# An SSD scan fused with a GELU feed-forward layer on one core: the scan regrouped into twelve units of 256 tokens, two tokens per partition, with 64-row tiles and Y written into the Gram banks

## The chip, the core and the metric

One core of one Trainium2 chip runs the whole program. The metric is the device time of one execution in microseconds (us); lower is better. Three plain runs of the kernel before took 124.39, 124.88 and 125.17 us, so the median is 124.88 us.

## The reference, cut to what matters

```python
batch, H, S, D = 4, 8, 768, 32      # N = d_state = 16, chunk = 32
log_a = np.log(np.clip(a, 1e-06, 1.0))
for c in range(S // chunk):         # xc, Bc, Cc, la: the chunk's slices
    cum = np.cumsum(la, axis=-1)
    L = np.exp(cum[..., :, None] - cum[..., None, :]) * causal
    M = np.einsum('bhin,bhjn->bhij', Cc, Bc) * L
    y_intra = np.einsum('bhij,bhjd->bhid', M, xc)
    y_inter = np.einsum('bhin,bhnd->bhid', Cc, state) * np.exp(cum)[..., None]
    y[:, :, sl] = y_intra + y_inter
    Bx = np.einsum('bhjn,bhjd->bhjnd', Bc, xc) * np.exp(cum[..., -1:] - cum)[..., None, None]
    state = np.exp(la.sum(-1))[..., None, None] * state + Bx.sum(axis=2)
h = y.transpose(0, 2, 1, 3).reshape(3072, 256) @ w_in        # w_in 256 x 2048
g = 0.5 * h * (1 + np.tanh(c * (h + 0.044715 * h * h * h)))
out = g @ w_out                                              # w_out 2048 x 256
```

Inputs and output are fp32. The result does not depend on the chunk length; both kernels use chunks of 128 tokens, 24 in all, six per batch.

## The kernel before

**Tiling.** The 24 chunks form 13 units (`UNITS`): chunks 0 and 1 alone, then eleven pairs, (2,3), (4,5) and so on. For each unit the kernel computes the scan's output Y, stores it transposed in bf16 as `xm` (256 features on partitions, tokens along the row), and runs the two layers on it: stage 1 (`f_s1`, matmul at L506) makes groups of 512 columns of `h` in one of two PSUM banks `hp`, `f_gelu` (ACT, L514) empties each into `gT`, and stage 2 (`f_s2`, L523) accumulates 128 tokens x 256 outputs over 16 slices of `gT`. `f_oev` empties the result and `f_store` (L536) stores 128 KB per chunk.

**The scan.** `f_R` scans the decay products, `f_RT0` and `f_RT` transpose them with fp32 matmuls (L282, L293), and `f_recip` inverts them. B and C are multiplied by these factors once per batch (`f_mul`, L349), transposed on TensorE (`f_T`, L358), copied from PSUM (`f_E`), C is masked by head parity (`f_F`, L373), and B is transposed back (`f_N`, L379). Per unit: `f_G` (L408) makes the products of B and C, 32-row tiles, into the four banks `gb`; `f_M` (L418, DVE) multiplies them with the triangle `tri`; `f_D` (L429) makes the state's increments in an `hp` bank; `f_S` and `f_SP` (L479, L486, DVE) carry the state and spread it over the heads; `f_Y` (L451 from the state, L460 from the products) accumulates Y in the bank `yb`, both in four 32-column tiles; `f_yev` (L469, ACT) empties it.

**Loads.** All but two loads are issued by SyncE's queue (SP) in one order: a, chunk 0's B and C, batch 0's B and C (768 KB), then x by chunk and the weights. B and C of a batch are loaded as 1,024 rows of 384 bytes, x as 1,024 rows of 128 bytes per chunk. The weights go through six buffers `wf`; the cast `f_wi` (L258 on POOL, L260 on DVE) also permutes the columns of `w_in`, `f_wo` casts `w_out`.

**Order.** Each operation is a `Node` with an estimated duration, its inputs, the PSUM buffers it takes and a priority. `run_order` lays the nodes out by these estimates; the program is emitted in that order, and each engine works through its own list in order. From unit `MERGE` = 4 on, Y of one unit and D and G of the next are one node, `f_YDG`. Stage 1 and 2 have the lowest priority, so they fill what the scan leaves free. Until the first stage-2 matmul, `idle` puts matmuls on zeros (`wz`, L776) where the order foresees an idle TensorE.

Of the kernel before, what the change touches and what calls it, by code (L numbers as in the profile page):

```python
# [8 lines left out]
FP32 = mybir.dt.float32  # L9
# [84 lines left out]
def kernel(  # L94
# [9 lines left out]
):  # L104
    nc = tc.nc
# [5 lines left out]
    R6 = CPB  # L111
    NCH = batch * CPB
    HC = CPB // 2
    HS = S // 2
# [4 lines left out]
    UNITS = [[0], [1]] + [[c, c + 1] for c in range(2, NCH, 2)]  # L119
    NU = len(UNITS)  # L120

    const = ctx.enter_context(tc.tile_pool(name="const", bufs=1))
    ld = ctx.enter_context(tc.tile_pool(name="ld", bufs=batch))
    wfp = ctx.enter_context(tc.tile_pool(name="wfp", bufs=6))
    ldx = ctx.enter_context(tc.tile_pool(name="ldx", bufs=NU))
    xpool = ctx.enter_context(tc.tile_pool(name="xpool", bufs=6))
    work = ctx.enter_context(tc.tile_pool(name="work", bufs=2))
    msb = ctx.enter_context(tc.tile_pool(name="msb", bufs=4))
# [3 lines left out]
    opool = ctx.enter_context(tc.tile_pool(name="opool", bufs=6))  # L132
# [6 lines left out]

    a_t = const.tile([64, HS], FP32, name="a_t")  # L140
    a_half = [bass.AP(tensor=a.tensor, offset=a.offset + i * HS, ap=[[S, batch * H], [1, HS]])
              for i in range(2)]
    XF, X16 = {}, {}
    U = [dict() for _ in range(batch)]
    bc0 = const.tile([128, 2, H, N], FP32, name="bc0")

    def load_bc0(i, q):
        q.dma_start(out=bc0[:, i], in_=(B, C)[i][0, :, 0:Q, :].rearrange("h p n -> p h n"))

    def load_bc(b, i):  # L150
        d = U[b]
        if "bc" not in d:
            d["bc"] = ld.tile([128, 2, H, R6 * N], FP32, name="bc_t")
        nc.sync.dma_start(out=d["bc"][:, i],  # L154
                          in_=(B, C)[i][b].rearrange("h (p r) n -> p h (r n)", r=R6))

    nc.sync.dma_start(out=a_t[0:32], in_=a_half[0])
    nc.scalar.dma_start(out=a_t[32:64], in_=a_half[1])
    load_bc0(1, nc.sync)
    load_bc0(0, nc.scalar)  # L160

    wz = const.tile([128, 512], BF16, name="wz")
    nc.vector.memset(wz, 0.0)
    warm = const.tile([128, 1], FP32, name="warm")
    nc.vector.memset(warm, 0.0)  # L165
    nc.scalar.activation(warm, warm, AF.Gelu_apprx_tanh)
    ends = const.tile([64, Q], FP32, name="ends")
    nc.vector.memset(ends, 0.0)
    nc.vector.memset(ends[:, Q - 1:Q], 1.0)
    ac = const.tile([64, HS + 1], FP32, name="ac")  # L170
    nc.vector.memset(ac[:, HS:HS + 1], 0.0)
    pe1 = const.tile([64, HC], FP32, name="pe1")
    pe2 = const.tile([64, 2 * batch, HC], FP32, name="pe2")

    idf = const.tile([64, 64], FP32, name="idf")
    nc.gpsimd.memset(idf, 0.0)
    nc.gpsimd.affine_select(out=idf, in_=idf, pattern=[[-1, 64]], compare_op=ALU.not_equal,
                            fill=1.0, base=0, channel_multiplier=1)
    ident = const.tile([128, 128], BF16, name="ident")
    make_identity(nc, ident)  # L180
    bmask = const.tile([128, H * D], BF16, name="bmask")
    nc.gpsimd.memset(bmask, 1.0)
    bm3 = bmask.rearrange("p (h d) -> p h d", h=H)
    nc.gpsimd.affine_select(out=bm3, in_=bm3, pattern=[[-N, H], [0, D]],
                            compare_op=ALU.is_ge, fill=0.0, base=0, channel_multiplier=1)
    nc.gpsimd.affine_select(out=bm3, in_=bm3, pattern=[[N, H], [0, D]],
                            compare_op=ALU.is_ge, fill=0.0, base=N - 1, channel_multiplier=-1)
    tri = const.tile([128, Q], BF16, name="tri")
    make_upper_triangular(nc, tri, val=1.0, diag=True)
    tri_b = tri.rearrange("p (o q t) -> p o q t", o=1, q=1).to_broadcast([128, 4, 2, Q])  # L190

    sel8 = const.tile([64, H], FP32, name="sel8")
    nc.vector.tensor_reduce(out=sel8, in_=idf.rearrange("p (b h) -> p h b", h=H),
                            op=ALU.add, axis=mybir.AxisListType.X)
    selp = const.tile([64, H, N], FP32, name="selp")
    nc.vector.tensor_copy(out=selp, in_=sel8.rearrange("p (h o) -> p h o", o=1)
                          .to_broadcast([64, H, N]))
    m8 = const.tile([64, 2 * batch], FP32, name="m8")
    nc.gpsimd.memset(m8, 1.0)
    nc.gpsimd.affine_select(out=m8, in_=m8, pattern=[[-H, 2 * batch]], compare_op=ALU.is_ge,  # L200
                            fill=0.0, base=0, channel_multiplier=1)
    nc.gpsimd.affine_select(out=m8, in_=m8, pattern=[[H, 2 * batch]], compare_op=ALU.is_ge,
                            fill=0.0, base=H - 1, channel_multiplier=-1)
    par = const.tile([128, 2], FP32, name="par")
    bmp = bmask.rearrange("p (g e d) -> p e g d", g=4, e=2)
    for e in range(2):
        nc.vector.tensor_reduce(out=par[:, e:e + 1],
                                in_=bmp[:, e, :, 0:1].rearrange("p g o -> p (g o)"),
                                op=ALU.add, axis=mybir.AxisListType.X)
    r_t = const.tile([64, HS], FP32, name="r_t")  # L210

    rt = const.tile([128, R6, batch * H], FP32, name="rt")
    pt = const.tile([128, R6, batch * H], FP32, name="pt")
    q0 = const.tile([128, H], FP32, name="q0")
    bc0s = const.tile([128, 2, H, N], BF16, name="bc0s")
    ce0 = const.tile([128, 2, Q], BF16, name="ce0")
    bh0 = const.tile([128, Q], BF16, name="bh0")
    pend = const.tile([128, NCH], FP32, name="pend")
    WF = {}
    w_in_sb = const.tile([128, 2, d_ff], BF16, name="w_in_sb")  # L220
    w_out_sb = const.tile([128, NF, d_model], BF16, name="w_out_sb")
    xm = const.tile([128, 2, n_tokens], BF16, name="xm")


    gb = ps1.tile([128, 4, 512], FP32, name="gb")
    yb = ps1.tile([128, 512], FP32, name="yb")
    y4 = yb.rearrange("p (c w t) -> p c w t", c=2, w=2)
    rp0 = yb[:, 0:H]
    T6 = [gb[:, 2 * i, 0:S // 2].bitcast(BF16) for i in range(2)]
    T6_0 = [yb[:, 0:S // 2].bitcast(BF16), T6[1]]  # L230

    T0, DT, MT, RP = {}, {}, {}, {}
    state = {}
    gts, ops, hps, outs = {}, {}, {}, {}

    def load_x(u):
        b, c = divmod(UNITS[u][0], CPB)
        XF[u] = ldx.tile([128, 2, H, D], FP32, name="x_t")
        for k in range(len(UNITS[u])):
            nc.sync.dma_start(out=XF[u][:, k], in_=x[b, :, (c + k) * Q:(c + k + 1) * Q, :]  # L240
                              .rearrange("h p d -> p h d"))
# [11 lines left out]

    def copy(eng, o, i):
        if eng == "ACT":
            nc.scalar.activation(o, i, AF.Copy)  # L256
        elif eng == "POOL":
            nc.gpsimd.tensor_copy(out=o, in_=i)  # L258
        else:
            nc.vector.tensor_copy(out=o, in_=i)  # L260

    def f_wi(q, k0, k1, eng):
        for k in range(k0, k1):
            copy(eng, w_in_sb[:, k, q * 512:(q + 1) * 512].rearrange("d (k p) -> d k p", k=4),
                 WF[("i", q)][:, k].rearrange("d (p k) -> d k p", k=4))

    def f_wo(q, eng):
        copy(eng, w_out_sb[:, 4 * q:4 * q + 4], WF[("o", q)])


    def f_clip(i0, i1):
        nc.vector.tensor_scalar(out=ac[:, i0:i1], in0=a_t[:, i0:i1], scalar1=1e-6, scalar2=1.0,
                                op0=ALU.max, op1=ALU.min)

    def f_R(k):
        nc.vector.tensor_tensor_scan(out=r_t[:, k * Q:(k + 1) * Q][:, ::-1],
                                     data0=ac[:, k * Q + 1:(k + 1) * Q + 1][:, ::-1],
                                     data1=ends[:, ::-1], initial=1.0,
                                     op0=ALU.mult, op1=ALU.max)

    def f_RT0():
        nc.tensor.matmul(out=rp0, lhsT=r_t[0:32, 0:Q], rhs=idf[0:32, 0:H], start=True, stop=True,  # L282
                         skip_group_check=True)

    def f_RT(r0, r1):
        if r0 == 0:
            RP[1] = psh.tile([128, 512], FP32, name="hp")[:, 0:R6 * batch * H] \
                .rearrange("p (r j) -> p r j", r=R6)
        r6 = r_t.rearrange("q (p r) -> q r p", r=R6)
        for r in range(r0, r1):  # L290
            for i in range(2):
                rs = slice(32 * i, 32 * i + 32)
# [4 lines left out]
    def f_recip0():  # L297
        nc.vector.reciprocal(q0, rp0)

    def f_rtc():  # L300
        nc.scalar.activation(rt, RP[1], AF.Copy)
# [511 lines left out]
```

## Time and profile before

| What | Value |
|---|---|
| Median of three runs | 124.88 us |
| Span of the profiled execution, first to last instruction | 122.8 us |
| Around the span (the median less the span; the profile prints no other time of its own) | 2.1 us |
| TensorE matmuls busy | 114.6 us, 1506 matmuls |
| ScalarE (ACT) busy | 74.9 us |
| VectorE (DVE) busy | 68.3 us |
| GpSimd (POOL) busy | 23.0 us |
| Mean granted TensorE clock | 0.972 of full |
| DMA packets | 40,591, of which 35,904 under 512 bytes |
| Last stage-2 matmul ends, last DVE copy begins | 119.10 us |

How to read the profile: PE is TensorE, PEld its weight loads, SPq the queue of SyncE. "L506" is line 506 of the kernel before. The "chain" follows the work that ended last back to its causes and lists start, length and what. The "timeline" merges neighbouring instructions of a kind and gives start, length, engine, line and shapes. The "windows" give busy time and counts (x) by stretch. Matmuls overlap, and the time one is said to last includes its way through the array, so rates are taken from the distance between starts, which is what the chain prints.

### The profile page before, as it was taken

How to read it: one execution, taken by the hardware profiler on the slowest of the kernel's cores; microseconds unless marked ns; L12 is line 12 of the kernel's file. 1: busy time of each engine (PE TensorE's matmuls, PEld its weight loads, DVE VectorE, ACT ScalarE, POOL GpSimd, SP SyncE). 2: the span in 40 equal slices, each digit the busy share in tenths (PEclk: the TensorE clock that was granted, in tenths of full speed). 3: DMA queues.
4: the chain of work that ended last, by engine and by line, in shares of the span. 5: the costliest groups of instructions: out<-in, count | busy, mean ns of one | idle time of the engine just before them, and what ended most of it. 6: DMA issues, size and time to landing. Idle time of an engine off the chain costs nothing.

```text
span 122.8 us, 3507 instructions
## 1 busy us (share of the span) xinstructions
PE 114.6 (93%) x1506; PEld 96.2 (78%) x1506; DVE 68.3 (56%) x116; ACT 74.9 (61%) x145; POOL 23.0 (19%) x38
## 2 busy tenths in 40 slices
PE   5899978989799999999999999999999999999970
PEld 5687747778678798787879889787878888888860
DVE  3897999968849888184979672475663000000110
ACT  4025536674676677656686777865768766786310
POOL 7206967750320160122000000000000000000000
PEclk9975699999999999999999999999999999999999
DMA  3999959989799899851101101101110111100121
GB/s 52 242 266 265 328 112 370 320 191 200 128 229 221 127 235 216 145 134 48 43 0 48 43 0 48 43 0 48 43 43 5 45 43 45 45 21 22 43 90 43
DMA packets 40591, 14.09 MB, mean 115 GB/s; under 512 B 35904, under 2 KB 39040, under 8 KB 40576
## 3 DMA queue, kind: packets, MB, share of 16 engines
q1 hardware_dynamic: 39488, 13.75, 46.4%
q8 instruction: 12, 0.20, 0.7%
q10 hardware_dynamic: 1088, 0.11, 0.7%
q14 instruction: 3, 0.02, 0.1%
HBM read 10.72 MB, written 3.15 MB: 113 GB/s over the span
## 4 chain that ended last, share of the span: by engine, by line
PE 70%; SPq 18%; DMA 5%; DVE 3%; issue 1%; DVEq 0%
PE o_ps L523 29%; PE hp L506 29%; SPq L240 7%; DMA bc_t<-in_B_dram 5%; SPq L252 5%; SPq L154 4%; PE yb L523 3%; SPq L248 3%; PE gb L408 2%; PE yb L451 2%; PE yb L460 2%; PE gb L358 2%; DVE ch L260 2%; PE gb L379 1%; DVE bc L349 1%
## 5 line engine op out<-in xcount | busy, mean ns | idle before, releaser
L514 ACT ACTIVATE gT<-hp 128x512 bf16<-128x512 f32 x96 | 53.6, 596 | 24.4 <-PE hp L506 24.2
L506 PE MATMUL hp<-xm,w_in_sb 128*128 128x256 bf16 (+1 forms) x416 | 53.7, 267 | 0.9 <-POOL w_in_sb L258 0.4
L523 PE MATMUL o_ps<-w_out_sb,gT 128*128 128x256 bf16 x352 | 47.3, 273 | 0.0
L506 PEld LDWEIGHTS <-w_in_sb 128*128 128x128 bf16 x416 | 37.6, 99 | 7.7 <-issue 2.0
L523 PEld LDWEIGHTS <-gT 128*128 128x128 bf16 x384 | 37.1, 98 | 4.8 <-issue 0.4
L418 DVE TENSOR_TENSOR m<-gb,tri 128x1024 bf16<-128x1024 f32 (+1 forms) x25 | 29.1, 1173 | 1.9 <-PE gb L408 1.8
L532 DVE COPY o_sb<-o_ps 128x256 f32<-128x256 f32 x2 | 0.8, 424 | 25.6 <-PE o_ps L523 25.6
L258 POOL CAST x<-x_t 128x512 bf16<-128x512 f32 (+1 forms) x12 | 8.5, 710 | 25.0 <-DMA x_t<-in_x_dram 20.1
L479 DVE SCALAR_TENSOR_TENSOR s_new<-s_new,pend,hp 128x64 f32<-128x64 f32 x16 | 4.5, 279 | 11.5 <-PE hp L429 11.2
L776 PE MATMUL o_ps<-wz 128*128 128x128 bf16 x77 | 8.9, 267 | 1.3 <-DVE warm L165 1.3
L530 ACT ACTIVATE o_sb<-o_ps 128x256 f32<-128x256 f32 x20 | 7.7, 385 | 3.8 <-PE o_ps L523 2.1
L486 DVE SCALAR_TENSOR_TENSOR sp_new<-s_new,pend,bmask 128x256 bf16<-128x256 f32 x20 | 10.0, 506 | 0.0
L469 ACT ACTIVATE xm<-yb 128x512 bf16<-128x512 f32 (+1 forms) x13 | 7.3, 564 | 4.3 <-PE yb L460 2.1
L258 POOL CAST w_in_sb<-wf 128x512 bf16<-128x512 f32 x6 | 7.0, 1193 | 7.0 <-DMA wf<-in_moe_w_in_dram 7.0
L776 PEld LDWEIGHTS <-wz 128*128 128x128 bf16 x77 | 6.5, 122 | 1.8 <-DVE warm L165 1.2
L460 PE MATMUL yb<-m,x 128*32 128x128 bf16 x192 | 6.3, 223 | 0.6 <-DVE m L418 0.6
L373 DVE TENSOR_SCALAR ce<-ch,par 128x768 bf16<-128x768 bf16 (+2 forms) x10 | 5.9, 634 | 0.8 <-ACT ch L256 0.8
L451 PE MATMUL yb<-ce,sp_new 128*32 128x128 bf16 x160 | 5.3, 221 | 0.0
L408 PE MATMUL gb<-ce,bh 32*128 32x256 bf16 x96 | 5.1, 278 | 0.0
L460 PEld LDWEIGHTS <-x 128*32 128x32 bf16 x192 | 3.8, 97 | 1.5 <-issue 1.5
L358 PEld LDWEIGHTS <-bc 128*128 128x128 bf16 x48 | 3.8, 110 | 1.3 <-issue 1.1
L258 POOL CAST w_out_sb<-wf 128x1024 bf16<-128x1024 f32 x4 | 4.4, 1112 | 1.5 <-DMA wf<-in_moe_w_out_dram 1.5
(72 smaller groups left out, 61.6 us busy)
## 6 DMA issues: line engine op xcount, KB each, us to landing
x_t<-in_x_dram SPq DMA_DIRECT2D x24, 128.0 KB, 4.5
out_dram<-o_sb SPq DMA_DIRECT2D x24, 128.0 KB, 1.7
wf<-in_moe_w_in_dram SPq DMA_DIRECT2D x4, 512.0 KB, 6.9
wf<-in_moe_w_out_dram SPq DMA_DIRECT2D x4, 512.0 KB, 6.0
bc_t<-in_C_dram SPq DMA_DIRECT2D x4, 384.0 KB, 4.4
bc_t<-in_B_dram SPq DMA_DIRECT2D x4, 384.0 KB, 5.4
bc<-in_B_dram ACTq DMA_DIRECT2D x1, 64.0 KB, 4.2
bc<-in_C_dram SPq DMA_DIRECT2D x1, 64.0 KB, 2.8
```

The costliest lines, as they stand in the source:

```text
L240: nc.sync.dma_start(out=XF[u][:, k], in_=x[b, :, (c + k) * Q:(c + k + 1) * Q, :] .rearrange("h p d -> p h d"))
L258: nc.gpsimd.tensor_copy(out=o, in_=i)
L408: nc.tensor.matmul(out=gb[:, g, 256 * k:256 * k + 256], lhsT=bh_of(gc)[32 * g:32 * g + 32], rhs=ce_of(gc)[32 * g:32 * g + 32], start=True, ...
L418: nc.vector.tensor_tensor(out=MT[gc][:, g0:g1], in0=gb[:, g0:g1, 256 * k:256 * k + 256] .rearrange("p g (e t) -> p g e t", e=2), in1=tri_b ...
L451: nc.tensor.matmul(out=y4[32 * j:32 * j + 32, k, w], lhsT=sp[:, 32 * h:32 * h + 32], rhs=ce_of(gc)[:, h % 2], start=first(j), stop=False, ...
L460: nc.tensor.matmul(out=y4[32 * j:32 * j + 32, k, w], lhsT=X16[u][:, k, 32 * h:32 * h + 32], rhs=m[:, h // 2, h % 2, :], start=first(j), st ...
L486: nc.vector.scalar_tensor_tensor(out=sp_new.rearrange("p (g d) -> p g d", g=4), in0=state[("s", gc)].rearrange("p (o d) -> p o d", o=1).to ...
L506: nc.tensor.matmul(out=hp[:, j * nt:(j + 1) * nt], lhsT=w_in_sb[:, kc, fi * 128:(fi + 1) * 128], rhs=xm[:, kc, t0:t0 + nt], start=(kc == 0 ...
L514: nc.scalar.activation(gts[u][:, i * per:(i + 1) * per, 0:nt], hps.pop((u, i)).rearrange("p (j t) -> p j t", j=per), AF.Gelu_apprx_tanh)
L523: nc.tensor.matmul(out=ops[gc], lhsT=gts[u][:, fi, tt * Q:(tt + 1) * Q], rhs=w_out_sb[:, fi, :], start=(fi == 0), stop=(fi == NF - 1), ski ...
L530: nc.scalar.activation(o_sb, ops.pop(gc), AF.Copy)
L776: nc.tensor.matmul(out=zb[:, 0:128], lhsT=wz[:, 0:128], rhs=wz[:, 0:128], start=True, stop=True)
```

## The change

The kernel is rewritten around 12 equal units of two chunks (256 tokens). A partition q of a unit holds tokens 2q and 2q+1, so partitions 0 to 63 hold the first chunk and 64 to 127 the second. What differs:

- Loads: B and C per unit (1,024 rows of 128 bytes, 128 KB each), x per unit (1,024 rows of 256 bytes, 256 KB), in the order a, B and C of unit 0, x of unit 0, then weights and unit 1 in turns, `w_out`, then units 2 to 11. Eight `wf` buffers in place of six. The output is stored per unit in rows of 2 KB, the last unit's in two halves.
- `f_wi` casts without permuting; stage 1 reads `w_in` with a step of four elements (`w_in_k`) and `xm` in four runs of 64.
- The scan: `f_mul`, `f_T` and the copies `f_EB` (DVE, now with the parity mask, on B) and `f_EC` (ACT) run per unit; `f_N` and its copy are gone. x is cast in two halves of 64 partitions into a zero-padded tile `xz`. `f_G` uses 32 x 64 tiles, 32 matmuls of 128 columns; `f_D` 8 matmuls of 128 columns into the bank `tb`; `f_Y` adds, for each half w of the heads, two 128 x 128 matmuls from the state and 16 matmuls in 64 x 32 tiles, into the first 128 columns of the Gram banks.
- Order: no merged node; Y of units 2 to 11 is one node; G of unit u waits for the copy of Y of the unit before. The decay factors of batches 2 and 3 are made later (`f_RT`, `f_pp` with i = 1). `idle` divides by 0.107 throughout.

```diff
+    UPB = CPB // 2
     NCH = batch * CPB
...
+    NU = batch * UPB
+    T = 2 * Q
+    P = Q // 2
...
-    wfp = ctx.enter_context(tc.tile_pool(name="wfp", bufs=6))
+    wfp = ctx.enter_context(tc.tile_pool(name="wfp", bufs=8))
...
+        (q or nc.sync).dma_start(out=BCF[u][:, i],
+                                 in_=(B, C)[i][b, :, k * T:(k + 1) * T, :]
+                                 .rearrange("h (q r) n -> q h (r n)", r=2))
...
+        nc.sync.dma_start(out=XF[u], in_=x[b, :, k * T:(k + 1) * T, :]
+                          .rearrange("h (q r) d -> q h (r d)", r=2))
...
+    nc.gpsimd.memset(xz[P:128, 0, 0], 0.0)
+    nc.gpsimd.memset(xz[0:P, 0, 1], 0.0)
...
+    for i in range(1, XB):
+        nc.gpsimd.memset(xz[P:128, i, 0], 0.0)
+        nc.gpsimd.memset(xz[0:P, i, 1], 0.0)
...
+    w_in_k = w_in_sb.rearrange("d k (q p j) -> d k q j p", q=4, j=4)
...
-            copy(eng, w_in_sb[:, k, q * 512:(q + 1) * 512].rearrange("d (k p) -> d k p", k=4),
-                 WF[("i", q)][:, k].rearrange("d (p k) -> d k p", k=4))
+        copy(eng, w_in_sb[:, k, q * 512:(q + 1) * 512], WF[("i", q)][:, k])
...
+    def f_EB(u):
+        BHE[u] = work.tile([128, 2, T], BF16, name="bhe")
+        for e in range(2):
+            nc.vector.tensor_scalar(out=BHE[u][:, e], in0=TT[(u, 0)], scalar1=par[:, e:e + 1],
+                                    scalar2=None, op0=ALU.mult)
...
+    def f_EC(u, eng):
+        CH[u] = work.tile([128, 2, 2, P], BF16, name="ch")
+        copy(eng, CH[u].rearrange("p r c t -> p (r c t)"), TT[(u, 1)])
...
+    def f_castx(u, c, eng):
+        ps = slice(P * c, P * c + P)
+        copy(eng, xz[ps, u % XB, c], XF[u][ps])
...
+    def f_G(u):
+        for e in range(2):
+            for r in range(2):
+                for g in range(4):
+                    gs = slice(32 * g, 32 * g + 32)
+                    for c in range(2):
+                        nc.tensor.matmul(
+                            out=gb[64 * c:64 * c + 64, g, (2 * e + r) * Q:(2 * e + r + 1) * Q],
+                            lhsT=BHE[u][gs, e, r * 128 + P * c:r * 128 + P * c + P],
+                            rhs=CH[u][gs, :, c], start=True, stop=True,
+                            tile_position=(32 * g, 64 * c), skip_group_check=True)
...
+    def f_D(u):
+        for r in range(2):
             for g in range(4):
...
+                    out=o[gs], lhsT=BC16[u][:, 0, r, 2 * g:2 * g + 2].rearrange("p h n -> p (h n)"),
+                    rhs=xz[:, u % XB, 0:n, 2 * g:2 * g + 2, r * D:(r + 1) * D],
+                    start=(r == 0), stop=(r == 1), tile_position=(0, 32 * g),
...
+    def f_Y(u, w):
+        for c in range(2):
+            gc = 2 * u + c
+            if gc % CPB:
+                nc.tensor.matmul(out=gb[:, 2 * w + c, 0:Q],
+                                 lhsT=state[("sp", gc - 1)][:, 128 * w:128 * w + 128],
+                                 rhs=CH[u][:, :, c], start=True, stop=False,
...
+        for r in range(2):
+            for c in range(2):
+                cs = slice(P * c, P * c + P)
+                for j in range(4):
+                    h = 4 * w + j
+                    nc.tensor.matmul(out=gb[32 * j:32 * j + 32, 2 * w + c, 0:Q],
+                                     lhsT=xz[cs, u % XB, c, h, r * D:(r + 1) * D],
+                                     rhs=MT[u][cs, h // 2, h % 2, r],
+                                     start=(r == 0 and (2 * u + c) % CPB == 0), stop=(r == 1),
+                                     tile_position=(64 * c, 32 * j), skip_group_check=True)
...
+        xr = xm[:, :, u * T:(u + 1) * T].rearrange("p w (c r t) -> p w r c t", c=2, r=2)
+        for j in range(2):
+            q, k = divmod(2 * i + j, 4)
+            for w in range(2):
+                nc.tensor.matmul(out=hp[:, j * T:(j + 1) * T], lhsT=w_in_k[:, w, q, k],
+                                 rhs=xr[:, w], start=(w == 0), stop=(w == 1))
...
+    lx(0)
+    lwi(0)
+    lbc(1)
+    lwi(1)
+    lx(1)
+    lwi(2)
+    lwi(3)
     for q in range(4):
+        lwo(q)
+    for u in range(2, NU):
+        lbc(u)
+        lx(u)
...
+        if u > 1:
+            ys = [add("PE", 0.5, f_Y2, u, deps=ms + [g] + xc + inter, prio=q + 2)]
...
+        g.takes("gram", *yevn[u])
+        if u >= 3:
+            Gn[u].deps.append(gpn[(u - 3, 4)])
...
+            RTb = add("PE", 1.3, f_RT, 1, 0, 1, 2, deps=[R1], prio=30)
...
-        n = int((t1 - t0 - 0.05) / (0.107 if t0 < 6.3 else 0.2 if 9.5 < t0 < 13.2 else 0.07))
+        n = int((t1 - t0 - 0.05) / 0.107)
```

## The prediction

> **What bounds the kernel now.** I read the page's busy shares first, then the chain in order of time, then the groups of the dense stretch, then the timeline of the start.
>
> ```profile
> PE   114.6 (93%) x1506; PEld 96.2 (78%) x1506; DVE 68.3 (56%) x116; ACT 74.9 (61%) x145; POOL 23.0 (19%) x38
> ...
> PEclk9975699999999999999999999999999999999999
> ```
>
> TensorE is the bound; DVE, ACT and POOL have slack on average. The chain shows what it does in the dense part (start, length):
>
> ```profile
> 55.40 0.87 PE o_ps L523 x8
> 56.27 0.23 PE yb L451 x8
> 56.50 0.11 PE yb L460 x8
> 56.61 0.11 PE yb L451 x8
> 56.72 0.11 PE yb L460 x8
> 56.83 0.06 PE hp L429 x8
> 56.89 0.33 PE gb L408 x8
> 57.22 0.54 PE hp L506 x4
> 57.76 0.87 PE o_ps L523 x8
> ```
>
> Eight stage matmuls take 0.87, so one takes 0.109 us. Eight 32-column matmuls of 128 columns take 0.11, four side by side. The first group after full-array matmuls takes 0.23, the Gram's eight take 0.33 for 0.22 of streaming, and the four stage matmuls behind it 0.54 for 0.44: each change of tile shape costs 0.10 to 0.12 us. Y, D and G of a unit cost 0.56 + 0.06 + 0.33 + 0.10 = 1.05 us with three changes. The transposes change no shape and cost their streaming, 0.33 for six.
>
> How late the dense part begins is read from the groups of instructions, by shape, in the window from 31.74, where the chain leaves a late load of B, to the end of the matmuls (shapes, count, busy, mean ns, idle before):
>
> ```profile
> L523 PE MATMUL o_ps<-w_out_sb,gT 128*128 128x256 bf16 x328 | 43.8, 273 | 0.0
> L506 PE MATMUL hp<-xm,w_in_sb 128*128 128x256 bf16 x324 | 43.8, 273 | 0.0
> ...
> L523 PE MATMUL yb<-w_out_sb,gT 128*128 128x256 bf16 x32 | 4.0, 273 | 0.0
> ```
>
> 328 + 324 + 32 = 684 of 768 full stage matmuls are left (64 of stage 1's are half long and count half): 74.7 us. TensorE runs without a break worth naming to 119.10, 87.4 us, so the scan of nine double units costs 12.7 us there, 1.41 each (1.05, a third of 1.0 for a batch's 18 transposes, and waits). Only 84 x 0.109 = 9.2 us of stage work is done in the first 31.74 us. Why so little:
>
> ```profile
> 10.04 2.13 POOL L258 CAST w_in_sb<-wf 128x512 bf16<-128x512 f32 x2 [5.85 <-DMA wf<-in_moe_w_in_dram]
> ...
> 12.37 5.90 SPq L252 DMA_DIRECT2D wf<-in_moe_w_out_dram  x4
> 12.44 2.16 POOL L258 CAST w_in_sb<-wf 128x512 bf16<-128x512 f32 x2 [0.26 <-DMA wf<-in_moe_w_in_dram]
> ...
> 17.14 1.46 POOL L258 CAST w_in_sb<-wf 128x512 bf16<-128x512 f32 x1 [0.92 <-DMA wf<-in_moe_w_in_dram]
> ```
>
> `w_in` lands from 10.04 because 768 KB of B and C go ahead; its permuting casts take over a microsecond per half; the third `w_out` load waits in SP's queue for one of six buffers (DMA falls to 73 GB/s in 15 to 17.5 us). Single-chunk units give TensorE little to do.
>
> **The change: the scan on TensorE.** Per unit, Y keeps its streaming: four state matmuls of 128 columns (0.22) and 32 small ones, eight tiles at once (4 rounds of 0.055, 0.22). But it changes shape four times (small, full, small, full again) where the old one shared its way out with D and G: 0.44 + 0.40. G streams 32 x 128 columns over eight tiles, 0.22; D doubles to 0.11 for the padding. G and D stand next to each other (same inputs but x): three changes, 0.30. Transposes: 4 x 0.055 = 0.22. Sum 0.84 + 0.63 + 0.22 = 1.69 us, against 1.05 + 0.33 = 1.38: **0.31 us a unit lost**, four changes less two transposes. With the 0.03 of waits that the dense part shows now (1.41 less 1.38), 1.72.
>
> No row shows more than four tiles at once. Bounds: eight at once (above), or four, which doubles G and the small part of Y, +0.44 a unit. I take eight: D's eight matmuls take 0.06, 7 ns each, so starts are no limit, and eight tiles are the same 128 rows and columns cut once more. The Trainium skill speaks against it: TensorE: Matmul & The Clock Gate, section on the larger per-matmul floors ("Wait — 56ns, not 53.3ns?"), sets starts at least about 25 ns apart however small the matmul. By that rule the 64 small matmuls of G and Y would take 1.6 us instead of 0.44, an estimate of +14 us in all. The row of eight in 0.06 says that the floor does not hold across tiles.
>
> **Strided weights.** Stage 1's 384 loads read `w_in` with a step of 8 bytes. No bf16 row shows one. Lower end nothing: a load of this shape lasts 99 ns (page, L506 PEld) beside a matmul of 109. Upper end from the only strided loads:
>
> ```profile
> 6.60 1.43 PEld L293 LDWEIGHTS hp<-idf,r_t 32*64 32x64 f32 x24
> ...
> 8.10 0.50 PEld L316 LDWEIGHTS hp<-pe,selp 64*128 64x128 f32 x2
> ```
>
> 24 loads of 64 fp32 columns, step 24 bytes, in 1.5 us: 62 ns each, 125 ns for 128 columns, 16 over 109: 384 x 16 = +6.1 us. I take nothing, the nearest row being L506's own. The Trainium skill, SBUF — State Buffer, Specifications (TRN2), says that reads keep full bandwidth while two of them fall into a 16-byte line, which 8-byte steps do; no run here shows it yet.
>
> **The start.** Bytes in their new order against the measured rates (280 GB/s in 5 to 12.5 us, about 350 in the stretches of weights, 208 in those of x): 0.57 MB by 5 us; x of unit 0 and `w_in` 0 by 7.1, unit 1 whole by 10.8, `w_in` 3 by 14, `w_out` 3 by 19.7, B, C of unit 2 by 21.0, its x by 22.2. B, C in 128-byte rows are as many packets for a third of the bytes; that cost is in the rate.
> Unit 0: a lands near 3.1 (issued 0.80, 2.0 to 2.3 to landing), scan and transposed factors as now until 4.5, two multiplications (0.29 for 128, 0.95 for 768, so 0.42), transposes, `f_EB` 0.75, G at 6.8, first half of M 1.2. POOL now sets six 512-wide memsets ahead of the x casts (0.20 for 128, 0.31 for 256, so 0.54 each, 3.2 us, less the old `tri` and `m`): casts of x end near 8.8, D 9.0, state 9.5 and 10.1, second M 10.7, Y 11.1, stage 1 from 11.6 (now 11.95). The memsets' delay is covered: `w_in` 1 to 3 are cast on POOL by 12, 14 and 15.5 (two plain halves of 0.61 each, the row of x), so stage 1 of unit 0 ends near 16.4 in any case; without that cover it would cost up to 2 us.
> Unit 1: G waits for the copy of Y at 11.6, M 2.4 and state 1.6 on DVE, Y 15.5, stage 1 from 16.4. From there TensorE has stage 1 of unit 1 and stage 2 of both, 96 x 0.109 = 10.5, and unit 2's scan, 1.7: full to 28.6. Unit 2 itself: C lands 21.0, multiplications, transposes, copies to 23.3, G, then DVE's M and state 3.2, Y from 26.8, copied at 28.8. So stage 1 of unit 2 is ready as the work runs out. What is late next, if unit 2 is, is TensorE itself, one for one. Everything later is loaded well ahead of its use (2.8 us of loading a unit at these rates, 8.7 of TensorE). The new wait of G for the copy of Y has stage matmuls queued behind it on TensorE; from unit 3 on G also stands behind the fifth stage-1 group of the unit three before, when that copy is long done, so only units 1 and 2 pay, and their wait is in the times above.
>
> At 28.8, 128 stage matmuls are done, 14.0 us; now it is 84 three microseconds later.
>
> **The sum.** 28.8 + 640 x 0.109 (69.9) + nine units x 1.72 (15.5) + the late factors (six pairs of the kind of L293, 0.7, the fp32 L316 pair 0.4, changes 0.2: 1.3) = 115.5. For holes in the start: TensorE idles 1.1 of 7.74 us in 24 to 31.74 (busy 6.64); the same share of 12.4 us would be 1.8, none 0; I take 0.8: 116.3, against 119.1. The tail stays (122.8 - 119.1 = 3.7: a DVE copy, a store of 128 KB), span 120.0; with the 2.1 by which the median exceeds the span, **122.1 us**. DVE (about 5.8 us a unit) and ACT (8 x 0.60 + 0.60 + 0.77 + 0.39 = 6.6) stay under 8.7 a unit; covered by that slack, they cost nothing. The clock is at half from 7.8 to 14.6 now (0.51 in 7.7 to 14.6); loads bind there, so sparser filler costs nothing until 16.4, and up to 0.8 if the slow stretch lasts to 18.
>
> **The rivals.**
> *Strided weights bind* (the other side). Place: each of 384 loads in stage 1. It decides from (124.9 - 122.1) / 384 = 7 ns over 109, so a load of 116. At the fp32 row's 125: 122.1 + 6.1 = 128.2. For: no bf16 row; against: 99 ns beside 109. Chance 0.13.
> *Four tiles at a time.* 12 x 0.44 = 5.3: 127.4. For: no row of eight; against: the tight starts. Chance 0.09.
> *Unit 2 late and the start in holes*: DVE in its order, or loads at 280 instead of 350 GB/s (3.1 MB, +2.2 us): 124.3. For: the start hangs on three engines in fixed orders, and DVE is full there (9.12 of 9.40 in 14.6 to 24). Chance 0.20.
> *The start is better still* (no holes, POOL earlier): 1.5 to 2 less, 120.4. Chance 0.13.
> The forecast has 0.45, with its own range 121.0 to 123.4.
>
> **How the numbers follow.** A measurement of this kernel tells about 1% from no change, so faster is below 123.6, slower above 126.1. Forecast and better start are faster but for 0.03 of the first: 0.55; of the late start 0.03 goes to faster, 0.14 to the same, 0.03 to slower; strided weights split 0.02 same, 0.11 slower; four tiles 0.09 slower. Faster 0.58, same 0.19, slower 0.23. The range 119.8 to 127.4 leaves the far strided case and the best starts out.
>
> **What would show it.** Right: L506-like starts 0.109 apart in stage 1 and stage 2 alike; small-tile rounds of 0.055 for eight matmuls; seven extra tenths per unit at changes of shape, scan 1.7 a unit; first stage 1 near 11.6, some 125 stage matmuls before 28.8; no stall of SP on `wf`. Wrong: stage-1 matmuls further apart than stage-2's, G over 0.4, or TensorE idle beyond 2 us between 16 and 30.

## The result and the profile after

The changed kernel is slower: 129.5 us median of four runs (128.75 to 129.93) against 125.03 us for the kernel before on the same chip, ratio 1.036 (95% interval 1.031 to 1.042). The forecast was 122.1 us, 119.8 to 127.4. The span of the profiled execution grew from 122.8 to 127.1 us. The last TensorE work ends at 123.70 us instead of 119.10; the tail behind it is 3.4 us (before 3.7). So the whole loss lies in what TensorE does up to there. A few executions of a program run over 1.5% above its fastest; the ratios leave these out, the medians do not.

The page of the changed kernel, busy times:

```profile
PE 117.3 (92%) x1847; PEld 99.6 (78%) x1847; DVE 66.5 (52%) x150; ACT 75.0 (59%) x153; POOL 27.1 (21%) x53
```

TensorE is still the bound, with 341 more matmuls. The chain of the changed kernel in its dense part (start, length, engine, tile, line, count; L460 is stage 2, L447 stage 1, L417 and L426 the state and product parts of Y, L338 transposes, L362 G, L386 D):

```profile
64.38 0.11 PE gb L417 x2
64.49 0.23 PE gb L426 x16
64.72 0.22 PE gb L417 x2
64.94 0.24 PE gb L426 x16
65.18 0.33 PE tb L338 x4
...
73.42 0.23 PE tb L386 x8
73.64 0.54 PE o_ps L460 x4
74.19 0.36 PE gb L362 x32
74.55 0.54 PE o_ps L460 x4
```

Sixteen product matmuls take 0.23, of which 0.11 is streaming: eight tiles do run at once (with four, the streaming alone would be 0.22). But every change of shape adds 0.11 to 0.13: Y pays it four times (0.23, 0.22, 0.24 and the 0.33 of the transposes behind it, which stream in 0.22). And in this unit D at 73.42 and G at 74.19 do not stand together: each pays its way in and out, the four stage matmuls behind each take 0.54 instead of 0.44. Counted over the trace from 31.74 on, TensorE changes shape 72 times; before it did 30 times.

The groups of instructions of the changed kernel by shape, window from 31.74 to the end of the matmuls (count, busy, mean ns, idle before):

```profile
L460 PE MATMUL o_ps<-w_out_sb,gT 128*128 128x256 bf16 x325 | 43.9, 273 | 0.5 <-ACT o_sb L258 0.5
L447 PE MATMUL hp<-xm,w_in_sb 128*128 128x256 bf16 x320 | 43.7, 274 | 0.0
...
L460 PE MATMUL gb<-w_out_sb,gT 128*128 128x256 bf16 x32 | 3.8, 273 | 0.0
```

677 stage matmuls are left at 31.74 (two of them under way), 7 fewer than before: the start gained 0.8 us, no more. The rest of the stretch, 123.70 - 31.74 - 677 x 0.109 = 18.2 us, is the scan with its changes of shape, and 0.5 us in which TensorE waits for ScalarE's copy of a result (the end of the first row; the wait ends at 116.46). The kernel before needed 12.8 by the same sum. The 42 changes more, at the 0.10 to 0.12 us that the experiments below give, are 4.2 to 5.0 of these 5.4 us.

The windows of the changed kernel, for the line of stage 1 and then for that of stage 2 (stretch, its length, matmuls busy and count, weight loads):

```profile
0.00:28.80 28.80, 8.71 (x53) 5.56 (x54) 0.94 0.92 228
0.00:28.80 28.80, 2.23 (x16) 1.57 (x16) 0.94 0.92 228
```

53 and 16: 69 stage matmuls by 28.8 us, where the prediction had 128. The timeline of the start says why:

```profile
4.80 3.33 SPq L171 DMA_DIRECT2D wf<-in_moe_w_in_dram  x1
...
13.52 0.66 DVE L262 CAST xz<-x_t 64x512 bf16<-64x512 f32 x1 [1.23 <-DMA x_t<-in_x_dram]
...
14.62 0.58 PE L362 MATMUL gb<-ch,bhe 32*64 32x128 bf16 x32
...
18.72 1.31 POOL L260 CAST w_in_sb<-wf 128x512 bf16<-128x512 f32 x2 [1.11 <-DMA wf<-in_moe_w_in_dram]
...
20.09 0.52 PE L447 MATMUL hp<-xm,w_in_sb 128*128 128x256 bf16 x3 [0.26 <-POOL w_in_sb L260]
20.44 0.28 PE L417 MATMUL gb<-ch,sp_new 128*128 128x128 bf16 x2
...
22.35 1.90 DVE L262 CAST w_out_sb<-wf 128x512 bf16<-128x512 f32 x4
...
23.09 1.04 PE L460 MATMUL o_ps<-w_out_sb,gT 128*128 128x256 bf16 x8
...
23.85 0.87 POOL L260 CAST w_out_sb<-wf 128x512 bf16<-128x512 f32 x1 [0.67 <-DMA wf<-in_moe_w_out_dram]
```

SP stands 3.33 us in one issue of `w_in`, behind the B and C of unit 1. The last quarter of `w_in` is cast from 18.72, the last of `w_out` from 23.85. G of unit 1 comes at 14.62, behind a cast of x on DVE that waited for its load (13.52). Y of unit 1, ready on DVE by 19.0, stands in TensorE's list behind the stage-1 group that waits for the last cast of `w_in` (20.44). Stage 2 begins at 23.09, behind DVE's casts of its share of `w_out` (from 22.35).

### The profile page after: what moved, and what is told of

Read it like the earlier page. It is cut to its first block, busy times and chain, and to the rows that moved or that the text cites. A ratio compares the mean times of both kernels' runs of the same rounds, so it can differ in the third digit from the quotient of the medians.

```text
span 127.1 us, 4249 instructions
## 1 busy us (share of the span) xinstructions
PE 117.3 (92%) x1847; PEld 99.6 (78%) x1847; DVE 66.5 (52%) x150; ACT 75.0 (59%) x153; POOL 27.1 (21%) x53
## 4 chain that ended last, share of the span: by engine, by line
PE 77%; SPq 10%; DMA 8%; DVE 1%; issue 1%; ACT 0%; DVEq 0%
PE hp L447 31%; PE o_ps L460 30%; DMA wf<-in_moe_w_out_dram 8%; SPq L171 4%; PE gb L426 4%; PE gb L362 3%; PE gb L460 3%; PE gb L417 2%; SPq L175 2%; PE tb L338 2%; SPq L163 2%; PE tb L386 2%; SPq L156 1%; PE hp L284 1%; DVE r_t L276 1%
## 5 line engine op out<-in xcount | busy, mean ns | idle before, releaser
L447 PE MATMUL hp<-xm,w_in_sb 128*128 128x256 bf16 x384 | 54.1, 277 | 1.8 <-POOL w_in_sb L260 1.2
L460 PE MATMUL o_ps<-w_out_sb,gT 128*128 128x256 bf16 x352 | 47.5, 273 | 0.5 <-ACT o_sb L258 0.5
L447 PEld LDWEIGHTS <-w_in_sb 128*128 128x128 bf16 x384 | 40.4, 115 | 4.9 <-POOL w_in_sb L260 2.4
L460 PEld LDWEIGHTS <-gT 128*128 128x128 bf16 x384 | 36.9, 98 | 5.1 <-issue 0.6
L371 DVE TENSOR_TENSOR m<-gb,tri 128x1024 bf16<-128x1024 f32 x23 | 27.9, 1220 | 11.7 <-PE gb L362 8.2
L260 POOL CAST xz<-x_t 64x512 bf16<-64x512 f32 x23 | 14.4, 626 | 36.8 <-issue 15.9
L258 ACT ACTIVATE xm<-gb 128x512 bf16<-128x512 f32 (+1 forms) x12 | 6.6, 561 | 5.4 <-PE gb L426 4.8
L344 DVE TENSOR_SCALAR bhe<-tb,par 128x256 bf16<-128x256 bf16 x24 | 7.3, 344 | 1.6 <-PE tb L338 1.6
L426 PE MATMUL gb<-m,xz 64*32 64x128 bf16 x384 | 7.4, 222 | 0.0
L399 DVE SCALAR_TENSOR_TENSOR s_new<-s_new,pend,tb 128x64 f32<-128x64 f32 x16 | 4.4, 273 | 4.3 <-PE tb L386 4.3
L417 PE MATMUL gb<-ch,sp_new 128*128 128x128 bf16 x40 | 6.3, 223 | 0.0
L328 DVE TENSOR_TENSOR bc<-bc_t,pt 128x256 bf16<-128x256 f32 x12 | 5.5, 460 | 0.4
L362 PEld LDWEIGHTS <-bhe 32*64 32x64 bf16 x384 | 3.4, 104 | 2.7 <-issue 2.1
L362 PE MATMUL gb<-ch,bhe 32*64 32x128 bf16 x384 | 5.3, 221 | 0.1
L426 PEld LDWEIGHTS <-xz 64*32 64x32 bf16 x384 | 3.3, 89 | 2.5 <-issue 0.5
```

The costliest lines, as they stand in the source:

```text
L344: nc.vector.tensor_scalar(out=BHE[u][:, e], in0=TT[(u, 0)], scalar1=par[:, e:e + 1], scalar2=None, op0=ALU.mult)
L362: nc.tensor.matmul(out=gb[64 * c:64 * c + 64, g, (2 * e + r) * Q:(2 * e + r + 1) * Q], lhsT=BHE[u][gs, e, r * 128 + P * c:r * 128 + P * c ...
L371: nc.vector.tensor_tensor(out=MT[u][:, 2 * w:2 * w + 2].rearrange("p g e r t -> p (g e) (r t)"), in0=GE.get((u, w), gb[:, 2 * w:2 * w + 2] ...
L417: nc.tensor.matmul(out=gb[:, 2 * w + c, 0:Q], lhsT=state[("sp", gc - 1)][:, 128 * w:128 * w + 128], rhs=CH[u][:, :, c], start=True, stop=F ...
L426: nc.tensor.matmul(out=gb[32 * j:32 * j + 32, 2 * w + c, 0:Q], lhsT=xz[cs, u % XB, c, h, r * D:(r + 1) * D], rhs=MT[u][cs, h // 2, h % 2, ...
L447: nc.tensor.matmul(out=hp[:, j * T:(j + 1) * T], lhsT=w_in_k[:, w, q, k], rhs=xr[:, w], start=(w == 0), stop=(w == 1))
```

## The experiments

Theory A: the loss is changes of shape, some 0.1 us each, and a start that gained almost nothing. Theory B: the start alone. Theory C: the many small matmuls are slow in themselves. Rivals from the prediction: strided weights, the memsets on POOL. All ratios are to the kernel before, run beside it on the same chip, with 95% intervals. Counts of stage matmuls done are by their starts; in the profile of the changed kernel 93 had started by 31.74.

**Fewer changes in Y.** From unit 2 on, all four state matmuls (`f_Yi`) first, then all 32 small ones (`f_Ys`):

```diff
         def f_Y2(u):
-            f_Y(u, 0)
-            f_Y(u, 1)
+            f_Yi(u, 0)
+            f_Yi(u, 1)
+            f_Ys(u, 0)
+            f_Ys(u, 1)
```

> The changed kernel, but in units 2 to 11 the four state matmuls of Y (full array) go first and all 32 small ones after them, so Y changes tile shape twice and not four times. Theory A (the loss is the price of shape changes in the dense part): 20 changes less, at the 93 ns by which the start after a change is late (203 against 109 ns) 1.9 us less: 129.5 becomes 127.6. Theory C (the many small matmuls themselves, or eight tiles, are slow): nothing changes, 129.5. Theory B (only the late weights matter): 129.5 too.

Measured 126.09 us, ratio 1.011 (1.008 to 1.015). 50 changes instead of 72 after 31.74, and 98 stage matmuls done there. So the 3.4 us against the first measurement hold a better start besides the fewer changes.

**The changed kernel again**, for a second execution to compare with, beside three edits that follow (Gram and D in one node, the memsets, B and C on ScalarE's queue):

> The changed kernel, unaltered, beside the next three, to tell how much of the 3.4 us of the grouped Y (126.1 against 129.5) was the edit. Theory A: the 21 shape changes that went are worth 2.0 us; then this kernel takes 128.1 to 128.6 here and the rest was how the weights happened to land. If the edit is worth all of it: 129.5.

Measured 128.46 us, ratio 1.031 (1.024 to 1.039). Its profiled execution had the last quarter of `w_in` cast from 16.14 instead of 18.72, 81 stage matmuls by 28.8 instead of 69 (windows of stage 1 and of stage 2), and a span of 125.7: the start differs by that much between executions of one program.

```profile
16.14 1.17 POOL L260 CAST w_in_sb<-wf 128x512 bf16<-128x512 f32 x2 [0.27 <-DMA wf<-in_moe_w_in_dram]
0.00:28.80 28.80, 9.12 (x60) 6.45 (x60) 1.00 0.95 233
0.00:28.80 28.80, 2.73 (x21) 2.12 (x22) 1.00 0.95 233
```

At 31.74 it had 98 done, as many as the grouped Y. Against it the grouped Y is worth 2.4 us for 18 fewer changes (68 to 50), 0.13 each; in the two profiles TensorE's work ends at 122.34 and 120.20, 0.12 each. Theory C, by which this edit changes nothing, fell.

**The kernel before with the new one's changes.** Its merged node cut, so that shapes alternate three times more in each of eight nodes:

```diff
             def f_YDG(u):
-                f_Y(u)
+                fresh = set()
+                f_Y(u, (0,), fresh)
+                f_G(u + 1, (0,))
+                f_Y(u, (1,), fresh)
+                f_G(u + 1, (1,))
                 f_D(u + 1)
-                f_G(u + 1)
```

> The kernel before, with the merged node of units 4 to 11 cut into six pieces: first chunk of Y, first of G, second of Y, second of G, then D. Same matmuls, same inputs, same operands; three shape changes more in each of eight nodes. Theory A: 24 x 93 ns = 2.2 us more, 125.0 becomes 127.3, all of it after 31.7 us. Theories B and C: 125.0, since no matmul is smaller and no load moves.

Measured 127.48 us against 124.97, ratio 1.019 (1.013 to 1.025); 54 changes instead of 30, same matmuls, same loads, and in both profiles 684 stage matmuls left at 31.74. 2.5 us for 24 changes is 0.10 each (0.07 to 0.13 by the interval); TensorE's work ends at 121.70 instead of 119.10. This is the cleanest test: the price of a change is shown, in the kernel that is not changed otherwise.

**G and D in one node**, on top of the grouped Y:

```diff
+        def f_GD(u):
+            f_G(u)
+            f_D(u)
...
+            g = Gn[u] = add("PE", 0.45, f_GD, u, deps=[mb, eb, ec] + xc, prio=q + 1)
...
-        d = Dn[u] = add("PE", 0.2, f_D, u, ...)
+        d = Dn[u] = g if u > 1 else add("PE", 0.2, f_D, u, ...)
```

> The grouped Y, and from unit 2 on G and D as one node, so that no stage matmul can come between them (it did in five of nine units). Theory A: 5 to 6 changes less, 0.5 us: 125.6. Against it: D now makes G wait for the casts of x on POOL; if those are late in units 2 and 3, up to 1 us is given back, 126.1 to 126.6.

Measured 124.92 us, ratio 1.002 (0.999 to 1.006), 1.2 us less than the grouped Y alone; its span is only 0.5 less (123.1 against 123.6), as the five changes saved would have it, so the size of this gain is less sure than its sign. The chain of this kernel:

```profile
44.73 0.22 PE gb L417 x4
44.95 0.35 PE gb L428 x32
45.30 0.56 PE hp L453 x4
```

Y is 0.22 + 0.35 with 0.12 on the stage matmuls behind it, 0.69 in all; in the changed kernel it was 0.80 + 0.11.

**The weights.** Only the first quarter of each weight matrix is loaded, the other casts read that quarter (3 MB of loads are left out; the edit for `w_in`, that for `w_out` is alike):

```diff
     def load_wi(q):
+        if q:
+            WF[("i", q)] = WF[("i", 0)]
+            return
```

> The changed kernel with only the first quarter of each weight matrix loaded and cast four times from there; the loads of the other six quarters (3 MB) are left out, all else and the order stay. It shows what the late weights cost. Theory B (the start failed to bring its gain because weights came 4 us late): stage 1 of unit 0 done near 16 instead of 20.6, TensorE nearly full from there, 5 us less: 124.5. Theory A alone, with the start bounded by DVE or by the order: 1 us less or none, 128.5 to 129.5. In both, the stretch from 32 us on keeps its 72 shape changes.

Measured 127.48 us, ratio 1.020 (1.015 to 1.025): 1.0 less than the changed kernel in its second measurement and 2.0 less than in its first, not 5. With the weights there in time, first stage 1 still comes at 12.98, Y of unit 1 at 19.22, first stage 2 at 21.95, no sooner than in the second execution of the changed kernel (12.98, 19.11, 21.76). DVE casts its share of `w_out` only from 21.21, though POOL's is done by 17.79. Theory B in this form fell: late weights are not the whole of the start.

**All of `w_in` ahead of unit 1:**

```diff
     lwi(0)
-    lbc(1)
     lwi(1)
-    lx(1)
     lwi(2)
     lwi(3)
+    lbc(1)
+    lx(1)
```

> The changed kernel with the four loads of w_in ahead of B, C and x of unit 1 in the queue. Theory B: w_in's last quarter is cast near 16 instead of 20, stage 1 of unit 0 ends sooner, unit 1 comes later by some 2 us than its own chain allows now (Y of unit 1 waits behind stage 1 of unit 0 at 20.4): 1 to 3 us less, 126.5 to 128.5. If the start is bound by the total of bytes and not by their order: 129.5 within 0.5.

Measured 132.85 us, ratio 1.064 (1.056 to 1.073). Unit 1 came later, and stage 2 only from 25.08: 76 stage matmuls at 31.74. Both expectations missed, though the last quarter of `w_in` was cast from 14.00; what is late next is the scan of unit 1, and everything that is listed behind it.

**The memsets on DVE** instead of POOL, on top of the grouped Y (one of two lines):

```diff
-        nc.gpsimd.memset(xz[P:128, i, 0], 0.0)
+        nc.vector.memset(xz[P:128, i, 0], 0.0)
```

> The grouped Y, with the four memsets of xz for the second and third buffer on DVE, which idles there, and not on POOL ahead of the casts of x. D of unit 0 waited 0.5 to 1.5 us for those casts. The prediction said that this delay is covered by the casts of w_in: then 126.1 within 0.4. If unit 0's chain sets the start: D at 7.5 and not 9.07, 1 to 1.5 us less, 124.8.

Measured 126.17 us, ratio 1.008 (1.004 to 1.012): the same as without the edit. D of unit 0 came at 8.47 instead of 9.07, the first mask product at 9.20 as before. The memsets are covered.

**B and C of unit 1 issued on ScalarE's queue**, on top of the grouped Y:

```diff
     load_a(1, nc.scalar)
+    load_bc(1, 0, nc.scalar)
+    load_bc(1, 1, nc.scalar)
...
+    bl[(1, 0)] = load(0.83, none)
+    bl[(1, 1)] = load(0.83, none)
     lx(0)
     lwi(0)
-    lbc(1)
     lwi(1)
```

The order takes these loads as earlier, so the edit also puts unit 1's multiplications ahead of unit 0's masks on DVE.

> The grouped Y, with B and C of unit 1 issued on ScalarE's queue at the start, so that SyncE's queue has neither them nor the 3.3 us in which it stood at the second w_in load. x of unit 1 and w_in 1 to 3 go out some 3 us earlier. If the loads' issue sets the start (theory B): stage 1 of unit 1 ready 1.5 to 2 us earlier, 124.2 to 124.8. If the packets themselves set it: 126.1 within 0.4, or up to 0.5 more, since unit 0's B and C share the engines with unit 1's.

Measured 125.15 us, ratio 1.001 (0.997 to 1.005): 0.9 less than the grouped Y. SP's first two issues of `w_in` take 2.12 together, where there they took 1.22 and 3.17, and the last cast of the weights on POOL comes 1.7 us earlier (20.94 for 22.65), with the same bytes and packets. One profile each can't show these 1.7 us to be the edit's: the casts of `w_in` moved by 2.6 between two executions of one program. 102 stage matmuls are done at 31.74 instead of 98, and G and D of one unit more.

**All three together:**

> The changed kernel with the three edits that gained by themselves: Y's state matmuls first, Gram and D as one node from unit 2 on, B and C of unit 1 issued on ScalarE's queue. If the three gains add up (1.2 and 0.9 us from the 126.1 of the first alone), 124.0 us. If the loads' gain only moves work that the fewer shape changes had already shortened, 124.6 to 124.9. First stage 1 near 13.4 and first stage 2 near 20.9, as with the loads' edit alone.

Measured 124.85 us, ratio 1.000 (0.996 to 1.004). The gains do not add up. 43 changes are left, but only 96 stage matmuls are done at 31.74. What came free on TensorE was not used at the start: DVE's casts of `w_out` came from 20.68 and stage 2 from 21.42.

**The same with DVE's old order**, unit 0's masks ahead of unit 1's multiplications:

```diff
+    lx(0)
+    lwi(0)
     bl[(1, 0)] = load(0.83, none)
     bl[(1, 1)] = load(0.83, none)
-    lx(0)
-    lwi(0)
     lwi(1)
```

> As the kernel with all three edits, but the order of the engines stays the one that the changed kernel had: only the queue of the two loads changes, DVE no longer takes unit 1's multiplications ahead of unit 0's masks. If the start hangs on the fixed order of DVE and TensorE in units 0 and 1, the first stage 1 goes back to near 11.9, Y of unit 1 comes 0.5 to 1.2 us earlier, and the time falls by as much: 122.8 to 123.5. If the landing of the weights sets the start whatever the order, no change against the kernel with all three: 124.0.

Measured 124.32 us, ratio 0.998 (0.994 to 1.002), not told apart from all three. First stage 1 came at 12.98 (13.61), but Y of unit 1 at 19.57 (18.77): what one unit gains on DVE the next loses. The earlier times of the first expectation did not come; no change is what the second one said.

**Weights with neighbouring columns** (the matching order of `w_out`'s rows is left out):

```diff
-  nc.tensor.matmul(out=hp[...], lhsT=w_in_k[:, w, q, k], ...)
+  nc.tensor.matmul(out=hp[...], lhsT=w_in_sb[:, w, f0:f0 + 128], ...)
```

> The changed kernel with stage 1 reading 128 neighbouring columns of w_in instead of every fourth; this leaves out the matching order of the hidden rows. If strided weight loads hide behind the matmuls, the same as the changed kernel, 128.0 to 128.9, with the mean load back from 115 to 99 ns. If they bind somewhere, by up to 16 ns in 384 loads, down to 122.3.

Measured 127.85 us, ratio 1.025 (1.017 to 1.033), the interval overlapping that of the unaltered kernel (1.024 to 1.039). The weight loads of stage 1, changed kernel:

```profile
L447 PEld LDWEIGHTS <-w_in_sb 128*128 128x128 bf16 x384 | 40.4, 115 | 4.9 <-POOL w_in_sb L260 2.4
```

and with neighbouring columns:

```profile
L447 PEld LDWEIGHTS <-w_in_sb 128*128 128x128 bf16 x384 | 35.9, 99 | 6.0 <-issue 0.2
```

The step of 8 bytes costs 16 ns a load, and eight stage-1 matmuls take 0.87 us in the chain all the same. Loads of 115 ns stay hidden behind matmuls that start 109 ns apart.

**All casts of `w_out` on POOL**, on top of all three:

```diff
-            e, t = ("POOL", 0.6) if k == 0 else ("DVE", 0.35)
+            e, t = "POOL", 0.6
```

> The kernel with all three edits, and all eight casts of w_out on POOL, where DVE had four of them behind unit 1's masks, states and copies. If stage 2 is late because DVE's share of the casts is late, first stage 2 comes near 18 to 18.5 instead of 21.4, four to eight stage matmuls of unit 0 fill the pauses of stage 1 before 21.4, and the time falls by 0.4 to 0.9: 124.0 to 124.4. If the start hangs on unit 1's chain alone, the same as all three: 124.8.

Measured 123.94 us against 124.59, ratio 0.994 (0.991 to 0.998): 0.6% below the kernel before, the one version whose interval lies below it. Its timeline, stage 2 on TensorE, and its windows for stage 1 and stage 2:

```profile
17.42 0.38 PE L468 MATMUL o_ps<-w_out_sb,gT 128*128 128x256 bf16 x2 [0.34 <-POOL w_out_sb L262]
18.17 0.38 PE L468 MATMUL o_ps<-w_out_sb,gT 128*128 128x256 bf16 x2 [0.37 <-POOL w_out_sb L262]
```

```profile
0.00:28.80 28.80, 8.34 (x59) 6.25 (x60) 1.00 0.98 236
0.00:28.80 28.80, 4.96 (x32) 3.05 (x32) 1.00 0.98 236
```

Stage 2 starts four microseconds earlier than with all three and 91 stage matmuls are done at 28.8, with 16 of stage 2 more than in the changed kernel. It waits for its weights even so, twice.

**Less work in DVE's row of unit 1**, on top of all three; the second mask product (1.22 us) is left out:

```diff
-              for w in range(1 if u == 0 else 2)]
+              for w in range(1 if u < 2 else 2)]
```

> The kernel with all three edits; unit 1's second mask product (1.22 us of DVE) is left out, and the second half of its Y reads the first half's masks. If DVE's chain of unit 1 (multiplications, copies, masks, states in one row) sets when TensorE gets full, Y of unit 1 comes 0.9 to 1.2 earlier than 18.8, first stage 2 near 20.2, and the time falls by 0.8 to 1.2: 123.6 to 124.0. If the casts of w_out or the pace of gelu set it, first stage 2 stays near 21 and the time near 124.8.

Measured 124.45 us, ratio 1.002 (0.999 to 1.005): no gain that the runs show. Y of unit 1 came 1.4 us earlier (17.38) and stage 2 at 19.62, somewhat more than the first expectation had, but the time stayed. Behind that comes a pause in which TensorE waits for DVE's multiplication of unit 2 (0.64 us before the transposes at 22.62), and this stands on DVE behind the last `w_out` cast, which itself waits for its load. The row of unit 1 alone does not set the time; a gain of some 0.3 us would not show in these intervals.

## Why the prediction was wrong, point by point

**The bound and the price of a change of shape: right.** TensorE set the end throughout, and a change costs 0.10 (the kernel before with 24 more) to 0.12 (the grouped Y), as the 0.10 to 0.12 read from the chain.

**Eight tiles at once: right.** Y's 32 small matmuls in one go take 0.35, 16 of them 0.23: sixteen more take 0.12, some 7 ns each. The floor near 25 ns between starts, which the page TensorE: Matmul & The Clock Gate of the Trainium skill states (section on the larger per-matmul floors), does not hold for tiles side by side in these runs. The rival "four tiles at a time" fell.

**"The change: the scan on TensorE", 1.69 (1.72) us a unit: too small, about 1.1 us of the miss.** From 28.8 to 123.70 the 699 stage matmuls that were left cost 76.2 us and the rest 18.7, where the sum had 17.6 for scan (15.5), late factors and holes. The late factors were already done by then. Of the 18.7, 0.9 is Y of unit 2, which the sum had before 28.8, and 0.5 the wait for ScalarE's copy, which it did not have; the other 17.3 are 1.92 a unit. Two terms were off: "G and D stand next to each other" was true of four of the nine units, and a change in Y was 0.11 to 0.13 rather than 0.10.

**Strided weights: right.** They cost the kernel nothing that can be measured; the load itself grew from 99 to 115 ns. What the Trainium skill says of full bandwidth with two reads in a 16-byte line (SBUF — State Buffer, Specifications (TRN2)) agrees with the kernel's time, though not quite with the load's.

**"The start": this step failed; 59 of 128 stage matmuls by 28.8 were missing, 6.4 of the 7.4 us by which the matmuls ended later than summed.** In the second execution 47 were missing, 5.1 of 6.0 us. Three of its terms fell.
- *Bytes against measured rates*: `w_in` 3 "by 14" and `w_out` 3 "by 19.7" were cast from 18.72 and 23.85 (16.14 and 22.49 in the second execution). Rates were taken from other rows and the queue left out: one issue stood 3.33 us behind two loads in 128-byte rows, while the core moved 168 GB/s in 8 to 10 us. Moving those two loads off the queue was worth 0.9. Leaving 3 MB of weights out was worth 1.0 to 2.0, so late loads are the smaller part of the miss.
- *"TensorE full from 16.4"*: it took stage 2 as ready when gelu was done. Half of the `w_out` casts stand on DVE, behind unit 1's masks, states and copies, so stage 2 came at 23.09, and at 21.95 even with every load of `w_out` there. Putting them on POOL was worth some 0.7 (ratio 1.000 to 0.994, intervals that just overlap) and brought stage 2 to 17.42.
- *Y of unit 1 at 15.5*: it came at 20.44. Its M and states cost what was said (15.35 to 19.0, 3.7 us against 4.0), but G came three microseconds late: behind unit 0's masks and states on DVE, then a cast of x that waited for its load. Taking 1.22 us out of this row moved Y but not the time, so it does not bind alone: the casts of `w_out` on DVE come next.

The three edits and the casts took the time from 128.46 to 123.94 us, 2.4 of the 4.5 by the grouped Y alone. In the best version 37 of the 128 matmuls were still missing at 28.8. What would bring these, 4 us of TensorE, stays open: each single relief left the next row in its place.

**Right as well:** the memsets are covered; the tail stays. *Unit 2 late and the start in holes* was the rival that came, but sized at 2.2 us over the forecast, where 5.1 to 6.4 were missing. The range was too narrow because no rival took away more of the start's gain than these 2.2.

## What to carry to other kernels

Count the changes of tile shape in the order in which the matmuls are really issued; at 0.1 us each, four more a unit cost nearly as much as all of Y's streaming (0.44), and grouping like with like won back 2.4 us. When a start is to be filled sooner, follow each piece of work to the last of its inputs in the list of the engine that makes it (here a cast of the second weight matrix behind a scan's masks), not only to the input that one thinks of first. A load can be paid for by whatever stands behind it in the same queue; whether its short rows made the queue stand was not tried. And a start read from one profile needs a second one beside it: here two executions of one program differed by twelve stage matmuls.

## What the runs showed of the hardware that was not expected

In one stretch of the start the stage matmuls and fillers begin at half rate. In the changed kernel it reaches from 11.2 to 14.2 us: four stage-1 matmuls at 11.88 take 0.85 us to the next start instead of 0.44, and the granted clock of the profile is 0.50 in 12 to 14 us. In its second execution the starts are as far apart from 6.0 to 15.0, and the first stage 1 comes at 12.98; the windows give a granted clock of 1.00 there. So the stretch lies elsewhere in another execution, and the record of the clock does not show every slow one; the distance between starts does. The first rows are from the first execution, the others from the second:

```profile
11.88 1.06 PE L447 MATMUL hp<-xm,w_in_sb 128*128 128x256 bf16 x4
12.00:14.00 2.00, 2.00 (x16) 1.69 (x15) 0.77 (x3) 0.87 (x2) 1.27 (x3) 0.50 0.90 220
...
12.98 1.06 PE L447 MATMUL hp<-xm,w_in_sb 128*128 128x256 bf16 x4
12.00:14.00 2.00, 2.00 (x29) 1.56 (x30) 1.58 (x5) 0.66 (x2) 1.61 (x3) 1.00 1.08 343
```

The first mask product of unit 0 on DVE began at 8.43, when ACT's copy of the other two Gram banks had ended (7.3 and 1.02 long); in the second execution it began at 9.20, behind a copy ending at 9.10. The two touch different banks. Why was not tried.
